# Reordered weight loads, an on-chip x split and merged attention bursts at the start of an attention and feed-forward kernel

## The chip, the cores and the metric

The kernel runs on one core of a Trainium2 chip. The metric is the device time of one execution in microseconds (us). The core has five engines with a queue of instructions each: PE (TensorE: matmuls and transposes, with the weight loads shown apart as PEld), DVE (VectorE), ACT (ScalarE), POOL (GpSimd) and SP (SyncE, which here only issues DMA transfers; ACT issues some too). An engine runs its queue in order, and an instruction whose operand is not there yet holds up all that stand behind it on its engine. Unlike the other engines, TensorE runs at a granted clock, given here as a share of full speed.

## The reference

Sparse attention of 8 batches with 8 heads of 576 positions and 64 numbers each, then a feed-forward network with a cosine over the 4608 rows of the result. Heads 0 to 3 see the 32 positions up to their own (local); heads 4 to 7 see every 32nd position before their own and themselves (strided).

```python
rel = pos[:, None] - pos[None, :]
mask_local = (rel >= 0) & (rel < 32)
mask_strided = (rel >= 0) & (pos[None, :] % 32 == pos[:, None] % 32)
scores = np.where(masks[None], scale * np.matmul(q, k.transpose(0, 1, 3, 2)), -1e9)
attn = np.exp(scores - np.max(scores, axis=-1, keepdims=True))
attn = attn / (np.sum(attn, axis=-1, keepdims=True) + 1e-09)
x = np.matmul(attn, v).transpose(0, 2, 1, 3).reshape(4608, 512)
h = x @ w_in                     # 512 x 2048
out = (h * np.cos(h)) @ w_out    # 2048 x 512
```

The two weight matrices come as 64-bit floating point numbers and are turned into 32-bit ones on the chip, from their integer halves. All results are needed in 32-bit precision.

## The kernel before, in words

**Attention.** A batch is ten *units* of work: four strided ones (`strided`) and six local ones (`local`), each for two heads. A unit loads its q and k (tile `qk`) and `v` through SP's queue, and then goes through four steps: the *scores* S (PE, lines 264 and 307), the softmax (`softmax`), the *transposes* T of the normalized tile (lines 274, 323) with a copy to SBUF by ACT, and the *products* P with v (lines 283, 337) with a copy by ACT into `x_t` or `x_l`. The result goes by a DMA of ACT's queue to `xT`, a buffer in DRAM (lines 291, 356).

In batches 0 and 1 (`plain`) a bfloat16 matmul first puts the mask into the bank of the scores (line 200). The softmax is then, in this order: DVE's maximum (215) and subtraction (216), ACT's exp (228), DVE's row sum (237), DVE's addition of 1e-9 to the sums (238) and reciprocal (239), POOL's normalizing multiplication (241). Batches 2 to 7 use another form with the mask added by DVE and the exponential from two Silu evaluations (lines 219 to 235), which saves changes of ACT's tables; lines 237 to 241 are the same for both.

**Feed-forward.** The tokens are 12 *blocks* of 384, w_in's columns 16 *chunks* f of 128. Each matrix operand is split in two: a high part rounded to fp32r and the rest as a low part; a product is three matmuls (high with high, high with low, low with high). `hidden(j, f)` makes h of one block and chunk with 12 matmuls (line 381), takes h·cos h on ACT and DVE (387 to 394) and splits it (397 on ACT, 398 on POOL). `outer(j, f)` multiplies that with w_out's chunk in nine matmuls (line 405) and, at the last chunk, copies and stores the block (413 to 416). `outer` follows three chunks behind `hidden` (LAG). The input of a block is read by `load_x` (364): four DMA loads from `xT` on SP, a cast each on DVE (371), a subtraction each on POOL (372).

**Weights.** `load_weight` (116) loads one chunk of one matrix (512 KB) on SP, assembles the 32-bit numbers on DVE (130, 133, 139) with a scaling on ACT between (138), casts the high part on ACT (143) and subtracts on POOL for the low part `wi_l` or `wo_l` (144).

**The program's order.** First come batches 0 and 1 (20 units, numbered 0 to 19), set out in stages by `in_stages` (428) and `stage` (439): unit n's scores at stage n, its transposes and products two and three stages later. 38 matmuls on a tile of zeros (`keep_busy`, line 478, counts in `BUSY`) stand between them. Then blocks 0 and 1 run their chunks in turn, each chunk's weights loaded just ahead, and the first three chunks of block 2. Last comes the main part: blocks 2 to 11, with the attention of batches 2 to 7 in *bursts* (`burst`, 447) at chunks set by the table `KNOTS`. A burst is the transposes of unit n−2, the products of unit n−3 and the scores of unit n; products and scores are interleaved where the products are strided.

The order in which the code is written is not what stands on the engines: the framework moves instructions by a schedule of its own, except where a dependency forbids it. `in_turn` (161) adds such a dependency between each matmul and the one before, and so fixes PE's order; before the change it holds for batches 2 to 7 and for blocks 2 and up, not for the opening. Within the opening, a warm matmul is tied to the scores ahead of it, and a weight step of DVE to a step of an earlier chunk. A tile pool gives out `bufs` buffers of a name in turn; a new tile waits for the last reader of the old one, and a pool opened where another was closed takes its memory and waits for its users.

Of the kernel before, what the change touches and what calls it, by code (L numbers as in the profile page):

```python
# [70 lines left out]
def attention_cos_ffn(ctx, tc, qkl, vl, qkvs, w_in, w_out, eye, eye16, mask_l0, mask_l, mask_s, out):  # L71
# [97 lines left out]
    class Attention:  # L169
# [24 lines left out]
        def score_bank(self, mask):  # L194


            if self.plain:
# [2 lines left out]
                nc.tensor.matmul(  # L200
                    bank[:, :n * w].rearrange("p (t w) -> p t w", w=w), ident16, mask, start=True, stop=False,
                    skip_group_check=True,
                )
# [7 lines left out]
        def softmax(self, s, mask, n, w, pn=None):  # L211
# [25 lines left out]
            nc.vector.tensor_reduce(out=z[:, :n], in_=e, op=ALU.add, axis=AX.X)  # L237
            nc.vector.tensor_scalar(out=z[:, :n], in0=z[:, :n], scalar1=1e-9, scalar2=None, op0=ALU.add)
            nc.vector.reciprocal(out=z[:, :n], in_=z[:, :n])
# [1 line left out]
            nc.gpsimd.tensor_tensor(
                out=pn, in0=e, in1=z[:, :n].unsqueeze(2).broadcast_to([P, n, w]), op=ALU.mult
            )
            return pn
# [7 lines left out]
        def local(self, b, p, u):  # L252
            qk = self.ld.tile([P, QS + KS], F32, name="qk")
            nc.sync.dma_start(out=qk[:, :QKL], in_=qkl[b, p, u])
# [7 lines left out]
            def score(t, j):  # L262
                lo = STRIDE if u + t == 0 else 0
                self.scored = self.pe(nc.tensor.matmul(  # L264
# [16 lines left out]
            def product(t, j):  # L281
                at = t * P + 64 * (1 - j)
                self.pe(nc.tensor.matmul(  # L283
# [7 lines left out]
            nc.scalar.dma_start(out=xT[:, 2 + p, at:at + LU * QB], in_=x_t)  # L291

        def strided(self, b, p, u):
            real = min(SU, NG - SU * u)
# [1 line left out]
            nc.sync.dma_start(out=qk, in_=qkvs[b, p, u, :, :QS + KS])
# [9 lines left out]
            def score(t, i):  # L306
                self.scored = self.pe(nc.tensor.matmul(  # L307
# [7 lines left out]
            pn = next(self.pn_s)  # L315
            self.softmax(
                s_ps[:, :SU * GB].rearrange("p (t w) -> p t w", w=GB), mask,
                SU, GB, pn[:, :, :GB],
            )
# [315 lines left out]
```

## Time and profile before

| what | value |
|---|---|
| time before, median of 3 runs | 971.35 us (969.21, 971.35, 971.7) |
| profiled execution, its own time | 974.17 us |
| span of that execution in the trace | 972.4 us |
| mean granted clock of PE | 0.991 |
| matmuls of blocks' chunks (lines 381, 405), from | 57.44 us |
| warm matmuls (line 478) | 38, together 14.3 us of PE |
| PE busy in 0 to 12 us | 10.96 of 12.00 us |
| PE busy in 57.4 to 75 us | 14.90 of 17.60 us |
| PE busy in 800 us to the end | 168.67 of 172.40 us |

The span is the time from the first to the last record; all positions below are microseconds from its start. A row of the timeline has the start, the duration, the engine, the line of the kernel, the operation with the tile written and the tiles read, the shapes, a count where rows of one kind are put together, and in brackets the idle time ahead with what ended it. A row of waits has the waiting group, its releaser, the sum in us, the count and the longest. Busy time of PE does not tell a matmul at half clock from one at full clock: there the granted clock has to be read beside it.

### The profile page before, as it was taken

What the parts mean: (1) busy time and instruction counts of PE and PEld (TensorE: products, weight loads), DVE (VectorE), ACT (ScalarE), POOL (GpSimd) and SP (SyncE); (2) the same over time, 40 slices, a digit from 0 to 9 for tenths busy, and PEclk for the clock granted to TensorE, in tenths of its full rate; (3) what the DMA queues carried; (4) which work ended last, traced back from release to release, by engine and by line L of the source; (5) the groups of instructions that cost most, each with busy time, mean ns of one, the idle gap of its engine ahead of it and who ended that gap; (6) DMA issues with size and microseconds to landing.
All of it is one profiled execution on the core that took longest, in us unless ns stands there. A gap on an engine that the chain in (4) does not pass through costs nothing.

```text
span 972.4 us, 17730 instructions
## 1 busy us (share of the span) xinstructions
PE 959.6 (99%) x6890; PEld 836.8 (86%) x6890; DVE 445.6 (46%) x989; ACT 506.5 (52%) x1059; POOL 383.2 (39%) x418
## 2 busy tenths in 40 slices
PE   8989999999999999999999999999999999999998
PEld 4678899988888888888888888888888888888997
DVE  6687655445454444444444444434344443222222
ACT  3467777466555545555445544554454544433433
POOL 2466555434443434333333444433343333222221
PEclk9799999999999999999999999999999999999999
DMA  8765333122323322111213132212221310100000
GB/s 263 236 208 197 130 130 109 33 93 89 108 70 99 87 76 87 52 51 61 58 59 96 59 86 75 77 42 63 91 60 36 110 54 22 41 21 1 33 1 33
DMA packets 48228, 80.14 MB, mean 82 GB/s; under 512 B 5904, under 2 KB 33296, under 8 KB 48144
## 3 DMA queue, kind: packets, MB, share of 16 engines
q1 hardware_dynamic: 38208, 69.35, 23.0%
q10 hardware_dynamic: 9936, 9.65, 2.8%
q8 instruction: 54, 0.88, 0.4%
q14 instruction: 30, 0.25, 0.1%
HBM read 60.11 MB, written 18.87 MB: 81 GB/s over the span
## 4 chain that ended last, share of the span: by engine, by line
PE 91%; DMA 4%; ACT 1%; issue 1%; POOL 1%; DVE 1%; SPq 0%; ACTq 0%; POOLq 0%; DVEq 0%
PE h L381 41%; PE acc L405 40%; PE acc L283 2%; PE acc L264 2%; PE acc L307 2%; PE acc L337 1%; PE acc L274 1%; DMA x_lo<-xT 1%; PE acc L323 1%; DMA xT<-x_t 1%; PE acc L478 1%; DMA raw<-in_w_out 1%; DMA qk<-in_qkl 1%; DMA xT<-x_l 0%; DMA v<-in_vl 0%
## 5 line engine op out<-in xcount | busy, mean ns | idle before, releaser
L398 POOL TENSOR_TENSOR g_lo<-r,g_hi 128x384 fp32r<-128x384 f32 x192 | 198.6, 1034 | 404.2 <-issue 257.7
L381 PE MATMUL h<-x_hi,wi_h 128*128 128x384 f32 x768 | 265.7, 346 | 2.7 <-DVE r L394 2.7
L381 PE MATMUL h<-x_hi,wi_l 128*128 128x384 f32 x768 | 259.4, 338 | 0.0
L381 PE MATMUL h<-x_lo,wi_h 128*128 128x384 f32 x768 | 258.0, 336 | 0.0
L388 DVE SCALAR_TENSOR_TENSOR r<-r,h 128x384 f32<-128x384 int32 x192 | 106.2, 553 | 283.3 <-ACT r L387 259.5
L405 PE MATMUL acc<-wo_l,g_hi 128*128 128x512 f32 x576 | 226.9, 394 | 0.0
L405 PE MATMUL acc<-wo_h,g_hi 128*128 128x512 f32 x576 | 226.9, 394 | 0.0
L405 PE MATMUL acc<-wo_h,g_lo 128*128 128x512 f32 x576 | 226.1, 395 | 0.0
L391 ACT ACTIVATE r<-r,biases 128x384 f32<-128x384 f32 x192 | 118.3, 616 | 84.5 <-DVE r L388 82.1
L381 PEld LDWEIGHTS h<-x_hi,wi_h 128*128 128x128 f32 x768 | 144.4, 188 | 13.9 <-DVE r L394 3.2
L387 ACT ACTIVATE r<-h 128x384 int32<-128x384 f32 x192 | 93.5, 487 | 118.4 <-PE h L381 112.9
L381 PEld LDWEIGHTS h<-x_lo,wi_h 128*128 128x128 f32 x768 | 144.7, 188 | 5.9
L381 PEld LDWEIGHTS h<-x_hi,wi_l 128*128 128x128 f32 x768 | 144.5, 188 | 0.0
L394 DVE TENSOR_TENSOR r<-r,h 128x384 f32<-128x384 f32 x192 | 106.0, 552 | 83.1 <-ACT r L391 82.5
L397 ACT CAST g_hi<-r 128x384 fp32r<-128x384 f32 x192 | 98.3, 512 | 85.8 <-DVE r L394 84.9
L405 PEld LDWEIGHTS acc<-wo_h,g_lo 128*128 128x128 f32 x576 | 107.7, 187 | 26.3
L405 PEld LDWEIGHTS acc<-wo_l,g_hi 128*128 128x128 f32 x576 | 107.8, 187 | 18.0
L405 PEld LDWEIGHTS acc<-wo_h,g_hi 128*128 128x128 f32 x576 | 107.7, 187 | 18.0
L372 POOL TENSOR_TENSOR x_lo<-x_lo,x_hi 128x384 fp32r<-128x384 f32 x48 | 50.3, 1049 | 117.7 <-DVE x_hi L371 100.4
L230 ACT ACTIVATE e_sb<-t_sb,biases 128x288 f32<-128x288 f32 (+1 forms) x60 | 32.9, 549 | 92.1 <-POOL t_sb L222 92.0
L371 DVE CAST x_hi<-x_lo 128x384 fp32r<-128x384 f32 x48 | 21.0, 440 | 66.1 <-DMA x_lo<-xT 62.8
L222 POOL TENSOR_TENSOR t_sb<-t_sb,mx 128x288 f32<-128x288 f32 (+1 forms) x60 | 41.6, 694 | 7.2 <-DVE mx L221 5.7
(66 smaller groups left out, 852.9 us busy)
## 6 DMA issues: line engine op xcount, KB each, us to landing
qk<-in_qkvs SPq DMA_DIRECT2D x32, 324.0 KB, 3.6
qk<-in_qkl SPq DMA_DIRECT2D x48, 208.0 KB, 2.8
x_lo<-xT SPq DMA_DIRECT2D x48, 192.0 KB, 2.4
out<-o SPq DMA_DIRECT2D x36, 256.0 KB, 2.1
raw<-in_w_in SPq DMA_DIRECT2D x16, 512.0 KB, 4.5
raw<-in_w_out SPq DMA_DIRECT2D x16, 512.0 KB, 3.8
v<-in_vl SPq DMA_DIRECT2D x48, 144.0 KB, 2.7
xT<-x_t ACTq DMA_DIRECT2D x16, 288.0 KB, 3.2
```

The costliest lines, as they stand in the source:

```text
L222: nc.gpsimd.tensor_tensor(out=t, in0=t, in1=mx[:, :n].unsqueeze(2).broadcast_to([P, n, w]), op=ALU.subtract)
L230: nc.scalar.activation(out=e, in_=t, func=AF.Silu, bias=shift1, scale=0.0625)
L371: nc.vector.tensor_copy(out=hi, in_=raw)
L372: nc.gpsimd.tensor_tensor(out=lo, in0=raw, in1=hi.bitcast(F32), op=ALU.subtract)
L381: mm = nc.tensor.matmul(h, w[:, f, c], x[c], start=(i == 0), stop=(i == len(ops) - 1))
L387: nc.scalar.activation(out=k, in_=h, func=AF.Copy, scale=1.0 / (2.0 * math.pi), bias=0.25)
L388: red = nc.vector.scalar_tensor_tensor(out=r, in0=k, scalar=-2.0 * math.pi, in1=h, op0=ALU.mult, op1=ALU.add)
L391: sin = nc.scalar.activation(out=r, in_=r, func=AF.Sin, bias=quarter)
L394: nc.vector.tensor_tensor(out=r, in0=r, in1=h, op=ALU.mult)
L397: nc.scalar.copy(out=g_hi, in_=r)
L398: nc.gpsimd.tensor_tensor(out=g_lo, in0=r, in1=g_hi.bitcast(F32), op=ALU.subtract)
L405: mm = nc.tensor.matmul(acc[t], g[:, ts], w[:, f], start=(f == 0 and i == 0), stop=(f == NFC - 1 and i == 2))
```

## The change

It does four things; lines are those of before unless said otherwise.

- **Merged bursts in a fixed order.** The opening uses `burst` as the main part does, with transposes three units behind the scores (PLAIN_LAG) and products four behind. `in_turn` now holds for all its matmuls, the warm and mask ones too, so PE's order there is the code's. 29 warm matmuls are left, the last of them behind burst 5.
- **Weight loads.** The load of the n-th weight tile is put behind the `qk` load of unit 5 + 1.5 n on SP's queue, as long as there are units.
- **x of blocks 0 and 1 stays on chip.** `keep` splits a unit's output right from `x_t` or `x_l` into the blocks' operand tiles (`split_x`: a cast on DVE, a subtraction on POOL), in one or two pieces as the token ranges fall. Only tokens from 768 on go to `xT`. `load_x(0)` and `load_x(1)`, eight loads with eight casts and subtractions, are gone; 14 casts and 14 subtractions come in.
- **1e-9 in a column.** The tiles of exponentials are six constant ones with one more column, which holds 1e-9 and is never written; the row sum reads it with the others, and DVE's addition (238) goes, in all eight batches. The normalizing multiplication is in place for the strided units too.

The opening's attention pools and the operand tiles of blocks 0 and 1 are allotted as before otherwise; the main part's code is the same but for the column.

```diff
-LOADS = (12, 20)
-BUSY = (10, 6, 5, 3, 2, 2, 2) + 8 * (1,)
+WEIGHTS_AT, WEIGHTS_EACH = 5, 1.5
+PLAIN_LAG = 3
+BUSY = (10, 6, 5, 3, 2, 2, 1)
...
+    e_l = [const.tile([P, LU, KW + 1], F32, name=f"e_l{i}") for i in range(3)]
+    e_s = [const.tile([P, SU, GP], F32, name=f"e_s{i}") for i in range(3)]
+    for t in e_s:
         nc.gpsimd.memset(t, 0.0)
+    for t, w in [(t, KW) for t in e_l] + [(t, GB) for t in e_s]:
+        nc.gpsimd.memset(t[:, :, w:w + 1], 1e-9)
...
-        nc.sync.dma_start(out=raw.rearrange("p n w -> p (n w)"), in_=src)
+        load = nc.sync.dma_start(out=raw.rearrange("p n w -> p (n w)"), in_=src)
+        behind = int(WEIGHTS_AT + WEIGHTS_EACH * len(tiles))
+        tiles.append(load)
+        if behind < len(loads):
+            order(load, loads[behind], "units first")
...
-            nc.vector.tensor_reduce(out=z[:, :n], in_=e, op=ALU.add, axis=AX.X)
-            nc.vector.tensor_scalar(out=z[:, :n], in0=z[:, :n], scalar1=1e-9, scalar2=None, op0=ALU.add)
+            nc.vector.tensor_reduce(out=z[:, :n], in_=tile[:, :, :w + 1], op=ALU.add, axis=AX.X)
...
-            nc.scalar.dma_start(out=xT[:, 2 + p, at:at + LU * QB], in_=x_t)
+            keep(2 + p, at, x_t)
...
-                nc.scalar.dma_start(out=xT[:, p, b * S:(b + 1) * S], in_=x_t)
+                keep(p, b * S, x_t)
...
+    def split_x(x, hi, lo):
+        nc.vector.tensor_copy(out=hi, in_=x)
+        nc.gpsimd.tensor_tensor(out=lo, in0=x, in1=hi.bitcast(F32), op=ALU.subtract)
...
+    def keep(c, at, x):
+
+        end = at + x.shape[1]
+        for j in range(2):
+            lo, hi = max(at, j * TB), min(end, (j + 1) * TB)
+            if lo < hi:
+                split_x(x[:, lo - at:hi - at], *(part[c][:, lo - j * TB:hi - j * TB] for part in first[j]))
+        lo = max(at, 2 * TB)
+        if lo < end:
+            nc.scalar.dma_start(out=xT[:, c, lo:end], in_=x[:, lo - at:])
...
+    first = [x_operands() for _ in range(2)]
...
-            steps = in_stages(att.units(0) + att.units(1), ((0, 0), (20, 20)), 2)
+            units = att.units(0) + att.units(1)
+            bursts = in_bursts(units, range(len(units) + PLAIN_LAG + 1), PLAIN_LAG)
...
-                    chunk(0, f, x0, acc0)
+                    chunk(0, f, first[0], acc0)
```

What this does to the engines' queues is shown at three places. The numbers in the names (`pn_s_91`, `e_l_93`) tell buffers of one name apart. The first place is POOL where the weights of the first chunks come in, during the first batch. Before, `pn_s` and `e_sb` are the normalized tiles of strided and local units (line 241), `wi_l` and `wo_l` the low parts of weights (line 144):

```order
L241 TENSOR_TENSOR pn_s_92<-e_sb,z 128x6x54
L144 TENSOR_TENSOR wi_l<-bits,wi_h 128x512
L144 TENSOR_TENSOR wo_l<-bits,wo_h 128x512
L241 TENSOR_TENSOR pn_s_91<-e_sb,z 128x6x54
L241 TENSOR_TENSOR pn_s_92<-e_sb,z 128x6x54
L241 TENSOR_TENSOR e_sb<-e_sb,z 128x288
L144 TENSOR_TENSOR wi_l<-bits,wi_h 128x512
L144 TENSOR_TENSOR wo_l<-bits,wo_h 128x512
L241 TENSOR_TENSOR e_sb<-e_sb,z 128x288 x2
```

Of the change, from the fourth and last strided unit of the batch on, with `e_s` and `e_l` as the normalized tiles (now line 247), the weights' low parts at line 153 and the split of x at line 368:

```order
L247 TENSOR_TENSOR e_s_94<-e_s_94,z 128x6x54
L153 TENSOR_TENSOR wi_l<-bits,wi_h 128x512
L368 TENSOR_TENSOR x_lo<-x_t,x_hi 128x384
L368 TENSOR_TENSOR x_lo<-x_t,x_hi 128x192
L247 TENSOR_TENSOR e_l_91<-e_l_91,z 128x3x96
L153 TENSOR_TENSOR wo_l<-bits,wo_h 128x512
L247 TENSOR_TENSOR e_l_92<-e_l_92,z 128x3x96
L247 TENSOR_TENSOR e_l_93<-e_l_93,z 128x3x96
L153 TENSOR_TENSOR wi_l<-bits,wi_h 128x512
```

Before, two weight steps stand between the second and the third strided unit, and none before the first local one. Of the change, a weight step and two splits of x stand between the fourth strided unit and the first local one (`e_l_91`).

The second place is DVE late in the second batch, from the maximum of its first strided unit on. Before, 215 is the maximum, 216 the subtraction, 237 the sum, 238 the addition and 239 the reciprocal; 371 casts x:

```order
L215 TENSOR_REDUCE mx<-h 128x6
L371 CAST x_hi<-x_lo 128x384
L239 RECIPROCAL z<-z 128x3
L238 TENSOR_SCALAR z<-z 128x3
L216 TENSOR_TENSOR t_sb<-h,mx 128x324
L239 RECIPROCAL z<-z 128x3
L215 TENSOR_REDUCE mx<-acc_599 128x6
L237 TENSOR_REDUCE z<-e_sb 128x3
L216 TENSOR_TENSOR t_sb<-acc_599,mx 128x324
L215 TENSOR_REDUCE mx<-h 128x6
L238 TENSOR_SCALAR z<-z 128x3
L237 TENSOR_REDUCE z<-e_sb 128x6
```

Of the change, the same place, with 225 the maximum, 226 the subtraction, 245 the sum, 246 the reciprocal and 367 the cast of x:

```order
L225 TENSOR_REDUCE mx<-h 128x6
L226 TENSOR_TENSOR t_sb<-h,mx 128x324
L245 TENSOR_REDUCE z<-e_s_95 128x6
L367 CAST x_hi<-x_l 128x192
L246 RECIPROCAL z<-z 128x6
L225 TENSOR_REDUCE mx<-acc_583 128x6
L226 TENSOR_TENSOR t_sb<-acc_583,mx 128x324
L245 TENSOR_REDUCE z<-e_s_96 128x6
L367 CAST x_hi<-x_l 128x192
L246 RECIPROCAL z<-z 128x6
L225 TENSOR_REDUCE mx<-h 128x6
L226 TENSOR_TENSOR t_sb<-h,mx 128x324
```

Before, the maximum of a later unit stands between the steps of earlier ones. Of the change, each unit's four steps stand together, with a cast of 192 columns between, and no addition.

The third place is SP's queue where the loads of batch 2, the first of the main part, begin. Before, `raw` are weights (line 120), `qk` and `v` with `in_qkvs` strided units' loads (lines 296, 298):

```order
L120 DMA raw<-in_w_out 128x1024
L120 DMA raw<-in_w_in 128x1024
L296 DMA qk<-in_qkvs 128x648
L298 DMA v<-in_qkvs 128x384
L296 DMA qk<-in_qkvs 128x648
L298 DMA v<-in_qkvs 128x320
L120 DMA raw<-in_w_out 128x1024
L298 DMA v<-in_qkvs 128x384
```

Of the change, weights at line 125, block 2's x at line 377, the stores of blocks 0 and 1 at line 431, and the loads of batch 2 at lines 302 and 304:

```order
L125 DMA raw<-in_w_out 128x1024
L377 DMA x_lo<-xT 128x384 x4
L431 DMA out<-o 128x512 x6
L302 DMA qk<-in_qkvs 128x648
L304 DMA v<-in_qkvs 128x384
L302 DMA qk<-in_qkvs 128x648
L304 DMA v<-in_qkvs 128x320
L304 DMA v<-in_qkvs 128x384
L304 DMA v<-in_qkvs 128x320
```

Batch 2's first `qk` stood among the weights of the middle chunks, with 23 weight loads, the loads of block 2 and the six stores behind it. Of the change it stands behind all of them.

More of the change, by code (lines that the diff above doesn't have):

```diff
@@ L209, in score_bank, with softmax @@
             return self.kept[n]
-        def softmax(self, s, mask, n, w, pn=None):
+        def softmax(self, s, mask, n, w):
+            tile = next(self.e[n])
+            e = tile[:, :, :w]
             t = self.wk.tile([P, SU * GB], F32, name="t_sb")[:, :n * w].rearrange("p (t w) -> p t w", w=w)
@@ L253, in local @@
             qk = self.ld.tile([P, QS + KS], F32, name="qk")
-            nc.sync.dma_start(out=qk[:, :QKL], in_=qkl[b, p, u])
+            loads.append(nc.sync.dma_start(out=qk[:, :QKL], in_=qkl[b, p, u]))
             v = self.ld.tile([P, VS], F32, name="v", bufs=4)
@@ L314, in strided @@
             ], True
[L315 to L319, printed above, removed]
+            pn = self.softmax(s_ps[:, :SU * GB].rearrange("p (t w) -> p t w", w=GB), mask, SU, GB)
             yield
@@ L426, in accumulators, with in_bursts @@
         return [pool.tile([P, DM], F32, name=f"acc{t}") for t in range(NTT)]
-    def in_stages(units, knots, lag):
-        begun = np.interp(range(len(units)), [n for _, n in knots], [at for at, _ in knots]).astype(int).tolist()
-        steps = {}
-        for n, (at, unit) in enumerate(zip(begun, units)):
-            second = min([at + lag] + begun[n + 2:n + 3])
-            for stage in (at, second, second + 1):
-                steps.setdefault(stage, []).append(unit)
-        return steps
-    def stage(unit):
-        matmuls = next(unit)
-        if matmuls:
-            for matmul in matmuls[0]:
-                matmul()
-            next(unit, None)
+    def in_bursts(units, begun, lag):
+        bursts = {}
+        for k, at in enumerate(begun):
+            bursts.setdefault(at, []).append(
+                [units[m] if 0 <= m < len(units) else None for m in (k - lag, k - lag - 1, k)]
+            )
+        return bursts
     def burst(transposed, multiplied, scored):
@@ L472, in attention_cos_ffn, with keep_busy @@
             )
[L473 removed]
+            units = att.units(0) + att.units(1)
+            bursts = in_bursts(units, range(len(units) + PLAIN_LAG + 1), PLAIN_LAG)
             spare = ps.tile([P, 512], F32, name="acc2")
[L476 removed]
+            def keep_busy(n):
                 for _ in range(n):
[L478 removed]
+                    in_turn(nc.tensor.matmul(
                         spare[:64], warm, warm.unsqueeze(1).broadcast_to([P, 8, 64]), start=True, stop=True
[L480 to L494 removed]
+                    ))
+            keep_busy(BUSY[0])
+            for n in range(max(bursts) + 1):
+                for members in bursts[n]:
+                    burst(*members)
+                if n + 1 < len(BUSY):
+                    keep_busy(BUSY[n + 1])
         gp = ctx.enter_context(tc.tile_pool(name="gp", bufs=LAG + 1, side="right", reuse_waits="tile"))
@@ L530, in attention_cos_ffn @@
                 cur, acc = nxt, accumulators(ps_o)
-            for units in bursts.get(n, ()):
-                burst(*units)
+            for members in bursts.get(n, ()):
+                burst(*members)
             if f == LOAD_AT and j + 1 < NTB:
```

68 lines of the change are left out of this document (20 added, 48 removed).

## The prediction

> **What bounds the kernel now.** I read the page's busy shares first, then a table of windows over the span, then who waited for whom on PE, and last the timeline where PE was not dense. In the windows the columns are PE, PEld, DVE, ACT and POOL busy, the granted clock, the DMA share and GB/s.
>
> ```profile
> PE 959.6 (99%) x6890; PEld 836.8 (86%) x6890; DVE 445.6 (46%) x989; ACT 506.5 (52%) x1059; POOL 383.2 (39%) x418
> ...
> 19.80:23.20 3.40, 1.80 (x34) 1.19 (x30) 3.40 (x11) 1.96 (x5) 1.82 (x2) 1.00 0.88 272
> 23.20:36.80 13.60, 13.03 (x120) 8.83 (x120) 8.86 (x25) 5.34 (x14) 5.47 (x6) 0.50 0.76 256
> 36.80:57.40 20.60, 20.12 (x357) 15.19 (x356) 16.83 (x50) 11.24 (x31) 10.78 (x14) 1.00 0.78 232
> ...
> 67.50:71.00 3.50, 3.50 (x15) 3.06 (x17) 2.43 (x5) 2.67 (x7) 2.14 (x2) 0.51 0.54 155
> ...
> 75.00:200.00 125.00, 125.00 (x624) 112.17 (x623) 73.89 (x129) 84.14 (x157) 71.66 (x61) 1.00 0.34 118
> 200.00:800.00 600.00, 598.33 (x4579) 527.20 (x4578) 271.63 (x634) 315.55 (x682) 233.01 (x270) 1.00 0.24 73
> ```
>
> From 75 us on PE stands still for 1.7 us before 800 and for nothing before 200. What the change can win therefore lies ahead of 75 us, and any wait that it puts behind 75 us is paid in full. Ahead of it PE lost time in two ways: it waited, and after each long wait the granted clock was 0.50, for 13.6 us the first time and 3.5 us the second.
>
> ```profile
> PE h L381 <- DVE r L394: 2.7, 1, 2.7
> PE h L264 <- DMA qk<-in_qkl: 2.2, 1, 2.2
> ```
> ```profile
> 57.44 0.44 PE L381 MATMUL h<-x_hi,wi_h 128*128 128x384 f32 x1
> ...
> 71.27 0.44 PE L381 MATMUL h<-x_hi,wi_h 128*128 128x384 f32 x1
> 71.65 0.57 PE L283 MATMUL acc<-pt,v 96*64 96x64 f32 x12
> ```
> ```profile
> 67.49 3.23 PE h L381 x9
> ...
> 87.55 2.10 PE h L381 x12
> ```
>
> I give the opening one number, its **dense point**: when the attention of batches 0 and 1 is done, less the FFN work done by then. The last attention products end at 71.65 + 0.50 = 72.15. By then 34 hidden matmuls have run (the first and the last are quoted), worth 34 x 2.10 / 12 = 5.95 us. So the dense point is 66.2 us, and a later or earlier one moves the end by as much.
>
> **The change, part by part: the opening up to unit 10.** Units are counted 0 to 19; S, T, P are a unit's scores, transposes and products.
>
> ```profile
> 12.01 0.31 PE L200 MATMUL h<-ms,ident 128*128 128x324 bf16 x1
> ...
> 26.56 1.23 PE L264 MATMUL acc<-qk 64*64 64x96 f32 x12
> ...
> 48.91 0.91 PE L337 MATMUL acc<-pt,v 54*64 54x54 f32 x24
> ...
> 53.16 0.71 PE L264 MATMUL acc<-qk 64*64 64x96 f32 x12
> ```
> ```profile
> 519.48 0.33 PE acc L323 x3
> ...
> 520.65 2.29 PE h L381 x12
> ```
>
> Interleaving strided products with scores is already done behind 200 us: transposes, products and scores took 520.65 - 519.48 = 1.17 us there, where products (0.91) and scores (0.71) one after the other take 1.6 without the transposes (0.33). With a mask matmul (0.31 at 12.01) a burst of the changed opening lies between 1.5 and 2.3 us; I take 1.8, nearer to the row of mixed work, and nine warm matmuls fewer are issued. The 2.2 us wait for qk goes too, since three units' qk now stand ahead of the weights in SP's queue. But PE is not what sets the pace any more: POOL is, and then DVE.
>
> ```profile
> 28.00 1.27 POOL L144 TENSOR_TENSOR wi_l<-bits,wi_h 128x512 fp32r<-128x512 f32 x1 [1.18 <-ACT wi_h L143]
> ...
> 32.96 0.67 POOL L241 TENSOR_TENSOR e_sb<-e_sb,z 128x288 f32<-128x288 f32 x1
> ...
> 37.22 1.00 POOL L372 TENSOR_TENSOR x_lo<-x_lo,x_hi 128x384 fp32r<-128x384 f32 x1 [2.58 <-DVE z L239]
> ```
> ```profile
> 21.56 0.68 DVE L133 SCALAR_TENSOR_TENSOR bits<-raw,bits 128x512 int32<-128x512 int32 x1
> ...
> 36.79 0.35 DVE L371 CAST x_hi<-x_lo 128x384 fp32r<-128x384 f32 x1
> ...
> 53.22 0.82 DVE L371 CAST x_hi<-x_lo 128x384 fp32r<-128x384 f32 x1 [0.21 <-DMA x_lo<-xT]
> ```
>
> PE reaches the transposes of unit 0 at 12.01 as now. From there in its new order, at 1.8 a burst and 0.1 to 0.3 for warm matmuls that are not covered (an estimate): S(4) ends at 15.6, S(5) at 17.7, S(6) at 19.6. T(4) comes next and needs unit 4's normalized tile, which on POOL now stands behind wi_l of the first chunk and two x_lo splits of unit 1's output. Their casts stand on DVE behind unit 5's subtract; ahead of that are a reduce, two weight steps and a sum, 0.45 + 0.6 + 0.6 + 0.4, with the subtract 2.4 us after S(5): 20.1. The casts end at 20.4 and 20.7; wi_l holds POOL to 20.9; two splits (1.0 and, half as wide, an estimate of 0.5) and the normalizing 0.67 give 23.1. **PE waits 3.5 us here** instead of 2.2. A drop of the clock is likely again: the window 19.80:23.20 with PE busy 1.80 of 3.40 us was followed by one. Then DVE has 7.5 us of work before unit 8 (eight weight steps, four casts, reduces, subtracts, sums), with three turns over ACT of 0.6, so unit 8's reduce starts near 29.5 and, two units later at 2.3, unit 10's at 34.1.
>
> ```profile
> 26.75 0.68 ACT L138 ACTIVATE raw<-raw 128x512 f32<-128x512 f32 x1
> ```
>
> Those turns are ACT's scaling between two weight steps of DVE. At half clock a burst takes 1.23 / 0.71 = 1.7 times as long, 3.1 us. Until about 32 us that lies beside PE's waits; beyond, I charge 1.1 us: 35.2, against 36.4 for the same reduce now (quoted next).
>
> **From unit 10 to the FFN** DVE's order is reduce, subtract, sum, reciprocal of one unit and then the next unit's, with ACT's exp in between, so one unit's chain is the period.
>
> ```profile
> 36.38 0.50 DVE L215 TENSOR_REDUCE mx<-h 128x6 f32<-128x324 f32 x1 [0.22 <-PE h L307]
> ...
> 59.22 0.45 DVE L215 TENSOR_REDUCE mx<-h 128x3 f32<-128x288 f32 x1
> ...
> 60.73 0.45 DVE L237 TENSOR_REDUCE z<-e_sb 128x3 f32<-128x288 f32 x1
> ...
> 61.22 0.17 DVE L238 TENSOR_SCALAR z<-z 128x3 f32<-128x3 f32 x1
> 61.42 0.18 DVE L239 RECIPROCAL z<-z 128x3 f32<-128x3 f32 x1
> ```
> ```profile
> L238 DVE TENSOR_SCALAR z<-z 128x3 f32<-128x3 f32 x12 | 3.8, 320 | 0.1
> L238 DVE TENSOR_SCALAR z<-z 128x6 f32<-128x6 f32 x8 | 3.4, 428 | 0.0
> ```
>
> Without the addition (L238, 3.8 + 3.4 = 7.2 us in all on DVE) the reciprocal starts where it started, at 61.22, and the next reduce 0.1 later: 2.1 us a local unit, 2.3 a strided one. Four strided and six local ones make 21.8, and the casts between them 0.5 of their 1.4 (seven of 0.2; the rest lies in the wait for exp). Unit 19 is through at 35.2 + 22.3 = 57.5, against 61.6 now. Its normalizing (0.7) and T (0.4) end at 58.6. By then 11 hidden matmuls have run (1.9), two product groups are left (1.0), and the third group of hidden matmuls waits about 1.0 for the first cosine. The x DMA round trip is gone, so the 2.7 us wait and its 3.5 us of half clock have no source. **Dense point 58.6 - 1.9 + 1.0 + 1.0 = 58.7: a gain of 7.5.** Bounds: at no POOL wait and no clock loss 4.6 better. At the worst all 14 casts take as long as the longest cast now, 0.82 (at 53.22) for 0.35: 14 x 0.47 = 6.6 worse.
>
> The Trainium skill ("SBUF — State Buffer", "Who interferes with whom") says that a cast or tensor_scalar in VectorE's two-port mode and a GpSimd instruction lock each other out. By that the 0.32 and 0.43 us for three and six numbers are waits for POOL, which the reciprocal's 0.17 to 0.18 beside them agrees with, and the casts would pay up to the 6.6 above.
>
> **Behind the opening: the first loads of batch 2.** Its first qk and v now stand on SP ahead of all output stores; after the change SP has them behind the last weights, the x loads and the six output stores, and the first waits for stores 1, 3 and 5 besides.
>
> ```profile
> 197.03 10.46 SPq L416 DMA_DIRECT2D out<-o  x6
> 208.02 5.44 SPq L296 DMA_DIRECT2D qk<-in_qkvs  x2
> ```
> ```profile
> 204.48 0.69 DVE L413 COPY o<-acc 128x512 f32<-128x512 f32 x1 [0.26 <-PE acc L405]
> ```
> ```profile
> 207.25 0.74 PE acc L307 x24
> ```
> ```profile
> out<-o SPq DMA_DIRECT2D x4, 256.0 KB, 2.0
> qk<-in_qkvs SPq DMA_DIRECT2D x2, 324.0 KB, 3.2
> ```
>
> On the clock of before: the sixth store is issued by 207.5; the fifth, copied at 205.17, has landed by 207.5. The first qk goes out at 207.6 and lands 3.2 later, at 210.8. PE wants it at 207.2, its matmuls stand in a fixed order, and everything after them waits: **3.6 us lost**. A wait of that length leaves one window like the two that lost the clock; 3.5 us at half then cost 3.4 x (1 - 0.175 / 0.32) = 1.5 (nine hidden matmuls in 3.23 us, the first at more than the rest). Lost: 5.1; bounds 0 (a load that comes earlier than the row says) and 7.
>
> Behind that only the addition leaves (hidden beside a dense PE); the two PE waits for POOL there (the 1.7 us between 200 and 800) may go or double: 0, bounds 1.7 each way.
>
> **Sum:** -7.5 + 5.1 = -2.4 us. The profiled execution took 974.17 us (span 972.4), 2.8 above the median of the runs, 971.35; by it 971.8 is due, on the median **969.0 us**.
>
> The Trainium skill ("TensorE: Matmul & The Clock Gate", "What's actually happening") says that a busy window of about 3.4 us brings the full clock back. The 3.5 us at 67.50 agree; the 13.6 us from 23.20, with PE busy 13.03, do not, so rows are used. By the rule the opening's loss of 1.1 goes and the time is 967.9.
>
> **The rivals.** (1) *Only the gain*: the qk of batch 2 does not hold PE up, or DVE's chain runs with less between its parts, net 5 to 12: about 963. For it: the 2.7 and 2.2 us waits and their clock go for certain. Against: SP's order. (2) *Slower, by the clock*: no warm matmul stands behind burst 6, and the half clock that the 3.5 us wait brings lasts to the FFN. Twelve bursts from 25.0 at 3.1 end at 62.2; the rest 3.3 x 1.7 = 5.6, the cosine 1.0, FFN at half 1.5: dense point 70.3, 4.1 worse, with the 5.1 it is 980.5. It decides from about 23 us of half clock on: each burst beyond costs 0.85. For it: 13.03 of 13.60 busy did not end it early. Against: the window 36.80:57.40, with the same kind of work, ran at 1.00. (3) *Slower a little*: the casts take most of their 6.6, the wait of batch 2 stays: about 974. (4) *The order is not what runs*: excluded, the rows are the program's.
>
> **How the numbers follow.** Forecast (net +1 to -6) 0.50, rival 1 0.24, rival 2 0.10, rival 3 0.16. A measurement here tells 0.3%, 2.9 us, from no change. Faster by more: 0.22 of the forecast's half and rival 1: 0.46. Slower by more: rival 2 and half of rival 3: 0.18. Within: 0.36. For 8 in 10, 961 to 975.
>
> **What would show it.** Right: PE waiting for POOL's normalizing at about 20 to 23 us; reduces of units 14 to 19 2.1 us apart; PE dense by 61 us; one wait of about 3.6 us for a qk DMA near 200 us, then 0.50. Wrong: no wait there, or a clock of 0.50 over most of 25 to 50 us.

## The result, and the profile after

The changed kernel took 977.26 us, median of 4 runs (976.02 to 978.58), against 971.27 of before (4 runs, 969.21 to 971.70): a ratio of 1.0066, interval 1.0039 to 1.0093. It is slower by 6.0 us where 2.4 less was forecast, and outside of the range. Its profiled execution took 976.02 us, with a span of 973.8.

The windows of the changed kernel (PE, PEld, DVE, ACT, POOL busy, granted clock, DMA share, GB/s), over the stretches shown of before:

```profile
19.80:23.20 3.40, 2.06 (x40) 1.50 (x38) 3.40 (x9) 3.05 (x9) 1.57 (x2) 0.52 0.85 248
23.20:36.80 13.60, 8.70 (x93) 6.34 (x94) 11.83 (x22) 6.82 (x16) 10.71 (x12) 0.50 0.62 187
36.80:57.40 20.60, 17.57 (x340) 13.29 (x342) 14.57 (x45) 10.23 (x30) 10.20 (x16) 0.91 0.73 231
67.50:71.00 3.50, 3.15 (x17) 2.96 (x18) 2.61 (x5) 3.50 (x9) 1.61 (x2) 1.00 0.37 103
75.00:200.00 125.00, 123.99 (x619) 111.14 (x618) 76.53 (x129) 83.88 (x156) 71.29 (x60) 1.00 0.32 109
200.00:800.00 600.00, 596.35 (x4564) 527.17 (x4563) 259.52 (x574) 315.13 (x680) 232.42 (x269) 1.00 0.25 75
```

The half clock behind the FFN's first chunk is gone, as forecast. But the one in the attention is longer (0.52 from 19.8 on, 0.50 to 36.8 and 0.91 on average behind), PE has only 8.70 of 13.60 us of work in it where it had 13.03, and DVE and POOL have more (11.83 and 10.71, before 8.86 and 5.47). Behind 200 us PE stands still for 3.65 us. The waits of PE:

```profile
PE acc L280 <- POOL e_l L247: 6.1, 4, 3.7
PE acc L313 <- DMA qk<-in_qkvs: 3.6, 1, 3.6
PE acc L325 <- POOL e_s L247: 3.4, 4, 1.9
PE h L396 <- DVE r L409: 1.9, 2, 1.0
```

Nine and a half us of the opening are waits for POOL's normalizing. PE's timeline at the first scores of batch 2:

```profile
209.82 0.81 PE L313 MATMUL acc<-qk 64*54 64x54 f32 x24 [3.65 <-DMA qk<-in_qkvs]
210.55 0.44 PE L396 MATMUL h<-x_hi,wi_h 128*128 128x384 f32 x1
...
214.14 0.56 PE L420 MATMUL acc<-wo_h,g_hi 128*128 128x512 f32 x1
```

The hidden chunk behind the wait takes 214.14 - 210.55 = 3.59 us in place of 2.10: 1.5 us to half clock. Together 5.15, where the prediction had 3.6 + 1.5 = 5.1. **The start of these scores, less the wait, measures the opening**, since PE is nearly dense up to there: 206.17 here, 207.18 before. By one execution of each the opening gained 1.0 us, not 7.5.

DVE in the opening, and two rows of POOL beside it:

```profile
16.70 0.43 DVE L139 TENSOR_SCALAR bits<-raw 128x512 int32<-128x512 int32 x1 [1.66 <-DMA raw<-in_w_in]
17.05 0.49 DVE L245 TENSOR_REDUCE z<-e_s 128x6 f32<-128x330 f32 x1
...
21.67 1.33 DVE L367 CAST x_hi<-x_t 128x384 fp32r<-128x384 f32 x2
...
25.84 1.64 DVE L142 SCALAR_TENSOR_TENSOR bits<-raw,bits 128x512 int32<-128x512 int32 x1
...
29.34 0.68 DVE L142 SCALAR_TENSOR_TENSOR bits<-raw,bits 128x512 int32<-128x512 int32 x1
...
33.75 1.27 DVE L367 CAST x_hi<-x_l 128x192 fp32r<-128x192 f32 x1
...
35.03 0.42 DVE L225 TENSOR_REDUCE mx<-acc 128x3 f32<-128x288 f32 x1
...
40.02 0.50 DVE L225 TENSOR_REDUCE mx<-h 128x6 f32<-128x324 f32 x1 [0.46 <-PE h L313]
...
61.88 0.18 DVE L246 RECIPROCAL z<-z 128x3 f32<-128x3 f32 x1
```
```profile
25.49 1.45 POOL L153 TENSOR_TENSOR wo_l<-bits,wo_h 128x512 fp32r<-128x512 f32 x1
26.90 1.11 POOL L247 TENSOR_TENSOR e_l<-e_l,z 128x288 f32<-128x288 f32 x1
```

One weight step takes 1.64 us while POOL works and 0.68 while it doesn't (28.87 to 30.15 us is a gap of POOL), a cast of 192 columns 1.27 where later ones take 0.23. Unit 8's maximum comes at 35.03; the prediction's sum had 29.5. Behind unit 10 the forecast pace holds, up to unit 19 at 59.88.

### The profile page after: what moved, and what is told of

Read it like the earlier page. It is cut to its first block, busy times and chain, and to the rows that moved or that the text cites. A ratio compares the mean times of both kernels' runs of the same rounds, so it can differ in the third digit from the quotient of the medians.

```text
span 973.8 us, 17615 instructions
## 1 busy us (share of the span) xinstructions
PE 952.3 (98%) x6881; PEld 834.2 (86%) x6881; DVE 435.7 (45%) x915; ACT 507.1 (52%) x1059; POOL 385.4 (40%) x431
## 4 chain that ended last, share of the span: by engine, by line
PE 92%; DVE 3%; ACT 1%; DMA 1%; POOL 1%; issue 1%; SPq 0%; ACTq 0%; DVEq 0%
PE h L396 42%; PE acc L420 41%; PE acc L289 2%; PE acc L270 2%; PE acc L313 2%; PE acc L280 1%; PE acc L339 1%; PE acc L325 1%; PE acc L486 1%; DVE z L245 1%; DVE t_sb L226 1%; DMA raw<-in_w_in 1%; DVE mx L225 0%; DVE bits L139 0%; ACT raw L147 0%
## 5 line engine op out<-in xcount | busy, mean ns | idle before, releaser
L368 POOL TENSOR_TENSOR x_lo<-x_lo,x_hi 128x384 fp32r<-128x384 f32 x40 | 41.6, 1042 | 104.7 <-DVE x_hi L367 75.0
L238 ACT ACTIVATE e_l<-t_sb,biases 128x288 f32<-128x288 f32 x36 | 19.4, 538 | 54.1 <-POOL t_sb L232 54.1
L367 DVE CAST x_hi<-x_lo 128x384 fp32r<-128x384 f32 x40 | 17.5, 440 | 57.3 <-DMA x_lo<-xT 53.9
```

What stands on the lines that cost most here:

```text
L368: nc.gpsimd.tensor_tensor(out=lo, in0=x, in1=hi.bitcast(F32), op=ALU.subtract)
```

## The experiments

Medians of e1 to e16 are those of 11 or 12 runs, ratios those to the kernel before on the same chip. It ran beside them in five groups (e1 to e4, e5 to e8, e9 to e12, e13 and e14, e15 and e16), with medians of 971.75, 970.68, 972.28, 971.58 and 971.32, so a difference of medians between two groups is uncertain by some 1 us more than its own noise. "Unit 8" is the start of its maximum, "batch 2" that of its first scores (less a wait for qk), "clock" the mean granted clock, all of one profiled execution. That of e11 lies 4.5 us below its median, that of e16 2.9 above.

| run | median us | ratio (95% interval) | unit 8 | batch 2 | clock |
|---|---|---|---|---|---|
| before (4 runs) | 971.27 | 1 | 27.83 | 207.18 | 0.991 |
| changed (4 runs) | 977.26 | 1.0066 (1.0039 to 1.0093) | 35.03 | 206.17 | 0.987 |
| e1 | 972.34 | 1.0008 (0.9991 to 1.0026) | 34.59 | 205.99 | 0.991 |
| e2 | 977.31 | 1.0062 (1.0041 to 1.0082) | - | 205.18 | 0.992 |
| e3 | 969.48 | 0.9975 (0.9955 to 0.9995) | 24.61 | 203.33 | 0.992 |
| e4 | 967.18 | 0.9950 (0.9933 to 0.9968) | 31.59 | 201.68 | 0.998 |
| e5 | 972.69 | 1.0022 (1.0006 to 1.0038) | 34.76 | 205.61 | 0.987 |
| e6 | 968.28 | 0.9980 (0.9970 to 0.9990) | 32.88 | 202.58 | 1.000 |
| e7 | 969.64 | 0.9988 (0.9972 to 1.0003) | 30.50 | 201.35 | 0.993 |
| e8 | 969.49 | 0.9994 (0.9972 to 1.0015) | - | 205.37 | 0.995 |
| e9 | 967.32 | 0.9951 (0.9931 to 0.9970) | 31.97 | 201.16 | 0.998 |
| e10 | 972.37 | 1.0008 (0.9991 to 1.0025) | 28.67 | 204.51 | 0.996 |
| e11 | 977.79 | 1.0048 (1.0022 to 1.0073) | - | 207.27 | 0.996 |
| e12 | 968.36 | 0.9969 (0.9950 to 0.9989) | 30.21 | 201.54 | 0.996 |
| e13 | 972.81 | 1.0021 (1.0002 to 1.0041) | 35.06 | 205.83 | 0.991 |
| e14 | 966.76 | 0.9950 (0.9930 to 0.9971) | 30.65 | 199.44 | 1.000 |
| e15 | 970.51 | 0.9990 (0.9969 to 1.0011) | 34.64 | 204.56 | 1.000 |
| e16 | 970.74 | 0.9988 (0.9967 to 1.0010) | 32.05 | 205.75 | 0.984 |

### The wait at batch 2: e1 and e2

The pools account for it. The six new tiles of exponentials are constants, and leave 42.84 KB per partition for the rest, by the opening's pools (cv 16, ld 13.59, wk 13.06 and 0.19 free in the program's allocation). Later cv (16), the two output buffers `o` (4) and, from the other end, `gp` (12) and the main part's `ld` (11.06) want 43.06: the first `qk` overlaps an `o` by 224 bytes. So it has to wait for the stores, and stands behind them on SP. e1 takes 320 bytes away:

```diff
-    ml = const.tile([P, KW], BF16, name="ml")
+    ml = ml0[:, KW:2 * KW]
...
-            z = sm.tile([P, SU], F32, name="z")
+            z = mx
```

> The changed kernel with 320 bytes per partition less of constants and small tiles (the mask ml is a view of ml0, the sums go into the tile of the maxima); the order on PE, DVE and POOL in the opening stays, and on SP batch 2's first qk and v stand 30 places earlier, among the weights. Theory (the wait of 3.65 us near 206 us comes from qk sharing memory with the output buffers): the wait and the clock of 0.66 behind it go, 3.65 + 1.7 = 5.3 us less than the changed kernel, so 971 to 973, ratio to the kernel before 1.000 to 1.002; the opening as before. Rival (the place on SP's queue only moved the wait; with the loads early, something else holds the first burst of batch 2, such as the stores or a busy DMA): under 2 us won, 975 to 977.

In e1's allocation 96 bytes are left between the two. e2 makes such an overlap (256 bytes) in the kernel before, with an unused tile below `o`:

```diff
+            pad = stack.enter_context(tc.tile_pool(name="pad", bufs=1)).tile([P, 1280], F32, name="pad")
+            nc.gpsimd.memset(pad[:, :1], 0.0)
             op = stack.enter_context(tc.tile_pool(name="op", bufs=2, reuse_waits="tile"))
```

> The kernel before with a tile of 5 KB per partition, unused, below the output buffers of blocks 0 and 1; with it batch 2's first qk stands behind the six stores on SP's queue, as in the changed kernel, and nothing else of the opening moves. Theory (shared memory alone makes the wait): a wait of 3 to 4.5 us for a qk DMA near 207 us and half clock for some 3 us behind it, 4 to 6 us slower than the kernel before, 975 to 977. Rival (the wait needs something else of the change): no wait over 1 us, within 1 us of the kernel before.

In e1 SP issues the load at 70 us and PE doesn't wait; in e2 the wait is there. SP and PE of e1, then PE of e2:

```profile
70.29 0.33 SPq L302 DMA_DIRECT2D qk<-in_qkvs  x1
```
```profile
205.99 0.81 PE L313 MATMUL acc<-qk 64*54 64x54 f32 x24
```
```profile
208.75 1.36 PE L307 MATMUL acc<-qk 64*54 64x54 f32 x24 [3.57 <-DMA qk<-in_qkvs]
```

e1 takes 4.9 us less than the changed kernel, e2 5.6 more than before. Memory shared between two pools makes this term, by itself. What is left, e1 against before, is the opening and the waits for POOL behind it: 1.0008, no gain that can be told. All that follows is built on e1.

### Weights and casts on DVE: e3, e7, e10, e12

```diff
-            after = reduced[f - AHEAD] if 0 <= f - AHEAD < len(reduced) else None
+            after = reduced[f - AHEAD] if 0 <= f - AHEAD < len(reduced) else sums[LATE[f]] if f < len(LATE) else None
```

> e1 with DVE's first weight step of chunks 0 and 1 ordered behind the reciprocals of units 9 and 13. Theory A (weights and x splits crowd DVE and POOL at 15 to 35 us, and that made unit 10 some 5 us late): waits of 1.9 and 3.7 us near 18 and 22 us mostly gone, unit 10's maximum 3 to 6 us earlier, 3 to 6 us less than e1. Theory B (fewer warm matmuls lose the clock, which is what makes it late): the clock still drops near 19 us for 15 us or more, under 1.5 us won.

e7 casts x on ACT (`split_x` calls `nc.scalar.copy` from `keep`):

```diff
-        nc.vector.tensor_copy(out=hi, in_=x)
+        cast(out=hi, in_=x)
```

> e1 with the 14 casts of x in the opening on ACT in place of DVE. Theory A (DVE, crowded by weight steps and casts that POOL's work stretches, sets the pace of 16 to 37 us): unit 10's maximum 2 to 4 us earlier than in e1 (39.7), the pace behind it 2.1 a unit, 2 to 4 us less than e1. Rival (POOL's own work, which stays, sets it): less than 1 us earlier, within 1 us of e1.

With two chunks' weight steps put off (e3) unit 8 comes 10.0 us earlier, without the casts on DVE (e7) 4.1. e3 puts off ACT's and POOL's work on these weights too; e7 takes work from DVE alone and leaves POOL's. So DVE's load, with what POOL adds to it, sets the time up to there. e7's gain over e1 is 2.7 us by the medians, 1.9 by the ratios. e3 pays most of its own back when the steps come later: PE then waits 5.0 us at once for a normalized tile, and the clock goes down from 34 to 44 us. e12 loads the weights from unit 3 on (`WEIGHTS_AT` 3), e10 puts chunk 1's weights behind unit 14 on top of e9 (below):

> e1 with the first weight load behind the qk of unit 3 in place of unit 5 (and the others as much earlier). Theory (DVE's wait of 1.7 us for the first weight, with the row sum of unit 3 behind it, is what makes PE's first wait of 1.9 us and starts the loss of the clock): DVE does not wait for the load, the wait for the normalized tile of unit 3 is under 0.7 us, the clock holds some 2 us longer; 0.5 to 2 us less than e1. Rival (the load only comes to collide with the loads of units, or the weight steps crowd DVE earlier): within 0.5 us of e1 or slower.

> e9 with DVE's first weight step of chunk 1 ordered behind the reciprocal of unit 14. Theory A: the weight steps of chunk 1 leave DVE's stretch from 24 to 33 us, unit 10's maximum 1 to 3 us earlier than in e9, and as DVE sets the pace up to unit 19 they come back later only in part: 0.5 to 2 us less than e9. Rival: all of it comes back behind unit 14, within 0.5 us of e9.

e12 gained more than expected, 4.0 us. DVE's wait for the load fell to 0.66 us and PE no longer waits for unit 3's tile, as the theory had it; but PE waits as long for unit 2's, whose sum the earlier weight steps now hold up. The transposes of units 2 and 3, the third and fourth of the opening:

```profile
18.23 0.55 PE L325 MATMUL acc<-ident,e_s 128*128 128x128 f32 x3 [1.89 <-POOL e_s L247]
```
```profile
19.89 0.55 PE L325 MATMUL acc<-ident,e_s 128*128 128x128 f32 x3
```

So a wait of that length was moved, not removed. What changed is unit 8 (4.4 us earlier) and the half clock, which starts at 28 us in place of 22. e10 lost 5 us against e9: unit 8 came 3.3 us earlier, and the weight steps that were put off made PE wait 2.76 and 2.28 us at 50 and 54 us, with the clock at 0.50 behind them. So the place of the weight steps counts by the waits of PE that it leaves.

### The clock and the order: e4, e5, e6, e13, e15, e16

e4 puts warm matmuls where PE waits:

```diff
-BUSY = (10, 6, 5, 3, 2, 2, 1)
+BUSY = (10, 6, 5, 3, 2, 2, 8, 14, 4, 5, 4)
```

> e1 with 57 warm matmuls in place of 29 (10, 6, 5, 3, 2, 2, 8, 14, 4, 5, 4), so that PE is busy while it waits for the normalized tiles of units 3 to 8. Theory B (the clock): 1.00 all through, unit 10's maximum 3 us or more earlier, 3 us or more less than e1. Theory A (DVE and POOL set the pace): clock 1.00 too, but unit 10's maximum less than 1.5 us earlier and under 1.5 us won; slower by up to 2 us if the warm matmuls hold up bursts.

It took 5.2 us less than e1 at a clock of 1.00 up to 64 us. But the framework's schedule counts PE's work too, and moved a few steps of DVE, POOL and ACT: from unit 10 on the next maximum stands ahead of a sum, and around units 6 and 7 maxima, weight steps and a split of x change places. e5 and e6 take the first of these apart:

```diff
+                maxima.append(nc.vector.tensor_reduce(out=mx[:, :n], in_=s, op=ALU.max, axis=AX.X))
+                if len(maxima) - 2 >= PIPE_FROM:
+                    order(sums[-1], maxima[-1], "next maximum first")
```

> e1 with one constraint on DVE more: from unit 10 on the row sum of a unit stands behind the maximum of the next unit. All else of the opening up to unit 10 stands as in e1, with its 29 warm matmuls. Theory O (DVE's order, one unit's chain after the other with a wait for exp of 0.6 in each, is part of what was lost): unit 10's maximum as in e1 near 39.7, the maxima of units 10 to 19 then 1.8 to 2.0 us apart in place of 2.1 to 2.3, batch 2's first scores near 203 in place of 206, 2 to 3.5 us less than e1. Theory B (the clock alone): within 0.7 us of e1.

> e4, with its 57 warm matmuls, and with DVE held to one unit's chain after the other from unit 10 on (the maximum of a unit behind the row sum of the unit before), as e1 has it. Theory O: unit 10's maximum near 36.6 as in e4, then 2.1 to 2.3 us a unit, unit 19's near 56.5; 2 to 3.5 us less than e1 and 2 to 3 more than e4. Theory B (the clock alone makes the 5.2 us between e1 and e4): within 0.7 us of e4.

e5's pace was 2.05 us a unit in place of 2.27, and nothing came of it (972.69): in its trace PE waits 1.90 us at 69.43 for the FFN's first cosine, 1.0 more than in e1, and the clock is 0.64 from 69.4 to 74 us, where e1 has 1.00. e6 kept 4.1 of the 5.2 us by the medians; it is 1.1 above e4 (95% interval, from redrawing the runs of both, -0.2 to 1.9; so for the differences below), and 2.9 by the ratios. So the order from unit 10 on alone gives nothing, and is at most a part of what e4 won. e13 tried few warm matmuls (`BUSY` 4 and 3 behind bursts 5 and 6), which leave the order all but as it is:

> e1 with six warm matmuls more (four in place of one behind burst 5, three behind burst 6). Unlike in e4, POOL's and ACT's order is that of e1, and DVE's but for the maximum and the subtraction of unit 6, which stand one and two places later. Theory B (the clock by itself is worth the time): the wait of 1.9 us shrinks to about 1.2, and the clock goes down 1 us later or more; the mean clock of the runs rises from 0.984 to 0.991 by 0.002 or more, and the time falls with it, by 1 to 2.5 us, at the rate that the runs of e1 among themselves show (5 us per 0.01). Theory O (only the order that the schedule gives the other engines made e4's gain): within 0.7 us of e1.

The first wait shrank to 1.35 us, but the second stayed at 4.71 and took the clock with it: no answer. e15 and e16 therefore write the order down, from the other program, and hold it:

```diff
+    def hold():
+        for names in HELD:
+            steps = [made[n.rstrip("0123456789")][int(n[len(n.rstrip("0123456789")):])] for n in names.split()]
+            for a, b in zip(steps, steps[1:]):
+                order(b, a, "held order")
```

> e4's 57 warm matmuls, with the order of DVE, POOL, ACT and SP held to that of e1 through all 20 units. Against e1 only the 28 warm matmuls differ. Theory B (the half clock is what costs the time): clock 0.998 to 1.00, 967 to 969, 3.5 to 5 us less than e1. Theory O (the other engines' order made e4's gain): 971 to 973.

> e1's 29 warm matmuls, with the order of DVE, POOL and ACT held to that of e4 through all 20 units. Theory B: the half clock of e1 stays (0.984 to 0.992), 971 to 973. Theory O: 967 to 969, as e4.

| | order of e1 | order of e4 |
|---|---|---|
| 29 warm matmuls | 972.34 (e1) | 970.74 (e16) |
| 57 warm matmuls | 970.51 (e15) | 967.18 (e4) |

Neither theory is right alone: e4 lies 3.3 us below e15 (interval 2.1 to 4.3) and 3.6 below e16 (2.0 to 5.0), so that order and clock both count. By these medians the clock is worth 1.8 us in e1's order (0.7 to 3.5) and 3.6 in e4's, the order 1.6 with 29 warm matmuls (0.0 to 3.5) and 3.3 with 57. That each is worth more beside the other is not shown: the difference of 1.7 has an interval of -0.3 to 3.6, and e1 and e4 ran in another group than e15 and e16. What the traces show is that in e1's order DVE holds PE up anyhow: the maximum of unit 8 on DVE, in e1 and then in e15 (line 242 is the same step, shifted by the added code), and the windows of e15.

```profile
34.59 0.42 DVE L225 TENSOR_REDUCE mx<-acc 128x3 f32<-128x288 f32 x1
```
```profile
34.64 0.42 DVE L242 TENSOR_REDUCE mx<-acc 128x3 f32<-128x288 f32 x1
```
```profile
12.00:23.20 11.20, 11.06 (x165) 6.62 (x163) 9.27 (x24) 6.83 (x16) 4.17 (x5) 1.00 0.90 275
23.20:36.80 13.60, 9.03 (x111) 5.21 (x109) 11.80 (x23) 6.84 (x16) 10.32 (x12) 1.00 0.66 198
```

With the clock at 1.00 throughout, unit 8 comes at the same time as in e1, to 0.05 us. Up to there, in this order, the half clock costs nothing that can be told. Behind it e15 wins 0.6 us up to unit 10 (39.10 against 39.65) and 1.4 up to batch 2 (204.56 against 205.99).

### Combinations, and two tries on the kernel before: e9, e14, e8, e11

e9 has e4's `BUSY` and e7's casts on ACT; e14 has e12's `WEIGHTS_AT` 3 and `BUSY` (10, 6, 5, 3, 6, 2, 8, 5, 13, 4, 4).

> e4 (57 warm matmuls) with e7's casts on ACT. If the clock (B: 4 to 5 us between e1 and e4) and the crowding of DVE by casts (A: 2.7 us between e1 and e7) are separate losses, 965 or a little less, 6 to 8 us less than e1, and batch 2's first scores near 199. If they are the same loss seen twice (casts off DVE shorten the waits and so save the clock), within 1 us of e4, 966 to 968.

> e12 with more warm matmuls at its waits (10, 6, 5, 3, 6, 2, 8, 5, 13, 4, 4). If e12's gain over e1 (4.0 us) was the shorter stretch of half clock, the same loss that e4 took away in another manner: clock 0.998 to 1.00, 966 to 968, as e4. If e12's gain was DVE's wait for the first weight, a loss of its own: 962 to 965.

Both end where e4 does (967.32 and 966.76 against 967.18), at clocks of 0.998 and 1.00, though e4, e7 and e12 won 5.2, 2.7 and 4.0 us each. The gains do not add: they are in the main one loss taken away, each time in another way, a DVE and POOL stretch that makes PE wait, and the half clock behind the wait. A further gain of e14 over e4 of up to 1.8 us lies within the interval. **e4, e9 and e14 beat the kernel before by 0.5%** (0.3 to 0.7), e12 by 0.3% (0.1 to 0.5), e3 and e6 by some 0.2% (0.05 to 0.45 and 0.1 to 0.3); all of them beat the changed kernel.

e8 leaves the addition (line 238) out of the kernel before, e11 gives that kernel nine warm matmuls at its wait for qk (`BUSY` (10, 6, 5, 3, 2, 2, 2, 9) and seven of one):

> The kernel before without the addition of 1e-9 to the row sums in any batch (it leaves out that part of the computation). By the prediction's sum the 7.2 us that the 20 additions of the opening take on DVE, with the waits for POOL in them, are part of the chain: 2 to 5 us less than the kernel before. Rival (in the order of before the additions stand in DVE's waits for exp and for PE): within 1.5 us.

> The kernel before with nine warm matmuls in place of one behind the eighth unit's stage, where PE waits 2.2 us for a qk. Theory B: the clock of 0.50 from 23 to 37 us goes in most runs, the spread of the runs (967 to 976) narrows to its lower half, median 968 to 969.5. Rival (the clock of that stretch costs nothing, since DVE and POOL set the pace there): median within 1 us of the kernel before.

e8 is 1.2 us below the kernel before, within its interval (2.7 below to 1.5 above), as the rival had it; the 2 us at the theory's lower end are not excluded. In its trace PE waits longer for a transfer, 3.06 us:

```profile
35.87 1.36 PE L306 MATMUL acc<-qk 64*54 64x54 f32 x20 [3.06 <-DMA qk<-in_qkvs]
```

e11 came out the other way, slower by 0.5%: its schedule changed in the second batch too, and in its trace the clock went down at 16 us already, ahead of the added matmuls. It tells nothing of what the clock costs.

## Why the prediction was wrong, by its steps

**Right:** the price of batch 2's loads. 3.6 + 1.5 us were forecast, 3.65 + 1.5 were in the trace, and e1 and e2 give 4.9 and 5.6. The place on SP behind the stores, from which the prediction worked, was its reason; e1 and e2 add that shared memory put the load there. Also right: that PE waits for POOL at unit 4's tile (3.5 us forecast, 3.72 measured); the pace from unit 10 on, 2.1 and 2.3 us a unit forecast, 2.07 to 2.36 measured; the half clock at 67.5 us gone; and the 1.7 us of waits for POOL behind 200 us, kept as a bound, did go.

The loss of the opening can be followed step by step, forecast against trace:

| step of the prediction | forecast, us | changed kernel, us | late by |
|---|---|---|---|
| the casts of unit 1's output end | 20.7 | 23.0 | 2.3 |
| unit 4's tile is there, PE goes on | 23.1 | 25.6 | 2.5 |
| unit 8's maximum starts | 29.5 | 35.0 | 5.5 |
| unit 10's maximum starts | 35.2 | 40.0 | 4.8 |
| unit 19 is through DVE | 57.5 | 62.1 | 4.6 |
| dense point | 58.7 | 63.6 | 4.9 |
| gain, measured at batch 2's first scores | 7.5 | 1.0 | 6.5 short |

**Wrong: the step "unit 8's reduce starts near 29.5".** It came at 35.03, and all that follows is late by about as much. The prediction took DVE's steps at their short rows, weight steps at 0.6 to 0.68 and casts at 0.35. The groups of DVE from 12 to 36 us of the changed kernel (sum in us, mean ns, idle time ahead) show what they took:

```profile
L148 DVE SCALAR_TENSOR_TENSOR bits<-raw,bits 128x512 int32<-128x512 int32 x4 | 4.3, 1083 | 0.8 <-ACT raw L147 0.8
L142 DVE SCALAR_TENSOR_TENSOR bits<-raw,bits 128x512 int32<-128x512 int32 x4 | 3.7, 919 | 0.0
L367 DVE CAST x_hi<-x_t 128x384 fp32r<-128x384 f32 (+1 forms) x4 | 1.8, 500 | 0.0
...
L367 DVE CAST x_hi<-x_l 128x192 fp32r<-128x192 f32 x1 | 1.3, 1270 | 0.0
...
L139 DVE TENSOR_SCALAR bits<-raw 128x512 int32<-128x512 int32 x2 | 1.1, 565 | 1.7 <-DMA raw<-in_w_in 1.7
```

The ten weight steps took 9.1 us where 8 x 0.68 + 2 x 0.43 = 6.3 would do, the five casts 3.1 where 2 x 0.35 + 3 x 0.23 = 1.4 would: 4.5 us of stretching beside POOL. The wait of 1.7 us for the first weight load, which the change issues at 11.8 us in place of 7.2, with unit 3's sum behind it in DVE's queue, wasn't seen at all. The two, less 0.7 us that DVE waited less for ACT than the prediction allowed, make up the 5.5 us. Up to the end of unit 1's casts it was the wait, 1.7, and 0.7 on the two casts. From there to unit 8's maximum 12.0 us passed in place of 8.8: the six weight steps left took 6.5 for 3.8, the three casts 1.8 for 0.8, and the waits for ACT 1.1 for the 1.8 allowed. (The "eight weight steps, four casts" of the prediction do not match the code's order, which has six and three there; its 7.5 us is about what these and the unit's own steps take when nothing stretches them.)

The stretching stood in the prediction only as a bound on the casts (6.6 us), and in rival 3 with a chance of 0.16, which is the nearest in mechanism; it belonged into the sum, and on the weight steps too, which the trace of before had at 1.16 and 1.61 us. That it goes with POOL shows in all 18 traces together, over their first 80 us: the 89 weight steps of the scalar_tensor_tensor form with no POOL instruction beside them took 0.67 to 0.69 us, the 161 with one 0.64 to 1.65. The casts of 192 columns took 0.23 to 0.26 (67 of them) and 0.25 to 1.29 (43). The maxima and sums took 0.41 to 0.50 either way. No run takes POOL's work away by itself. The Trainium skill ("SBUF — State Buffer", "Who interferes with whom") says that a VectorE instruction with two SBUF inputs contends with a GpSimd instruction that reads SBUF, and that VectorE's two-port modes and GpSimd lock each other out. The weight steps, which read two SBUF tiles, agree: 1.64 against 0.68 us for one step, with POOL at work and not; no run here shows in which mode the casts ran.

**About right in price, wrong in length: the clock term of 1.1 us.** The prediction charged half clock only beyond 32 us. It lasted from 19.5 to 40, so one of its own signs of being wrong, half clock over most of 25 to 50 us, came true. Yet e15, set against e1, which has some 17 us of it, prices it in this order at 0.6 us at unit 10, where PE, not DVE, had become the last to come (40.02), 1.4 at batch 2 and 1.8 by the medians. So the half clock is not what made unit 8 late.

**Missing: a wait behind the opening.** The dense point, taken as in the prediction, is the end of the last products, 66.39 + 0.50, less 24 hidden matmuls (4.2 us), with the wait for the first cosine (0.9): 63.6, a gain of 2.6. A second wait for the cosine, at 81.69, which the kernel before does not have, takes 1.0 of it; 0.6 is not placed.

```profile
66.39 0.57 PE L289 MATMUL acc<-pt,v 96*64 96x64 f32 x12
67.85 0.44 PE L396 MATMUL h<-x_hi,wi_h 128*128 128x384 f32 x1 [0.90 <-DVE r L409]
```
```profile
81.69 0.44 PE L396 MATMUL h<-x_hi,wi_h 128*128 128x384 f32 x1 [1.00 <-DVE r L409]
```

**Wrong: the base.** The sum was made against an execution of 974.17 us and then carried over to the median, 2.8 lower, as it stood. But the executions of this kernel differ in how much half clock they have, and half clock was what the change was to remove. 148 runs of the kernel before, beside those of the experiments, show it (the clocks with 15 runs or more):

| mean clock | runs | median us | range |
|---|---|---|---|
| 0.989 | 15 | 975.6 | 974.5 to 976.4 |
| 0.991 | 15 | 973.7 | 972.6 to 976.3 |
| 0.993 | 21 | 972.8 | 970.7 to 974.3 |
| 0.995 | 18 | 971.4 | 969.7 to 973.6 |
| 0.996 | 36 | 970.1 | 967.9 to 971.6 |
| 0.998 | 26 | 969.4 | 967.4 to 971.6 |

The 13.6 and 3.5 us at half clock of the profiled execution are 8.6 us short of full clock, which is its 0.991; a run at 0.998 has room for 4 us at half clock in all. More than half of the runs (89 of 148) are at 0.995 or above, and have less of it to give back. e2, which leaves the code of the opening's attention as before, shows one such opening: its first half clock lasts some 3 us, and batch 2 comes at 205.18 in place of 207.18, earlier than in the changed kernel. The changed kernel's four runs, like the 12 of e1, have 0.991 at most: the change lost the good runs.

By the two traces, 1.0 us was gained in the opening, 5.15 lost at batch 2 and some 1.6 gained at the waits for POOL behind: 2.5 lost in all. The two profiled executions differ by 1.9 (976.02 and 974.17; their spans by 1.4), so up to 1.1 us is not placed. The rest of the 6.0 us lies in the choice of the executions: the profiled one was 2.9 above the median before and 1.2 below it after.

**Open:** which of the moved steps, around units 6 and 7 or from unit 10 on, gives e4's order its 1.6 to 3.3 us. And no run has the change's parts one by one: the x split without the new weight order, or the reverse, wasn't tried.

## What to carry to other kernels

Price a step by its duration beside the engines that will be busy with it, not by its shortest row; where a change puts work on DVE and POOL into one stretch, the stretching belongs into the sum. A constant tile more can move two pools onto each other, and a transfer onto a wait, far from the edit: after any change of sizes look at what the first loads of the next phase wait for. And before a trace is used as a base, see whether its own excess over the median is the very thing that the change removes.

## What the runs showed of the hardware

Waits of 2 to 5 us among small matmuls were followed by a clock of 0.50 for 7 to 20 us, though PE was busy for 13.03 of the 13.60 us that it lasted before the change. How long such a wait has to be is not settled here: 1.92 us in e5 was followed by half clock, 1.89 in e12 and 1.88 in e8 were not. Warm matmuls in the waits kept the mean clock at 0.998 or more in 34 of 35 runs (e4, e6, e15). Over the 148 runs of one program the time falls by 7.2 us for 0.01 of mean clock (correlation -0.91), so that most of its scatter, 967 to 980 us, goes with the clock. That rate is no price of the clock by itself: e15 raised the mean clock of the runs by 0.010 against e1, and gained 1.8 us.
